# A planner's DMA rate, a tie between weight loads, and the order of three engines

## The chip, the cores and the metric

The kernel runs on one core of a Trainium2 chip. The metric is the device time of the whole launch in microseconds, lower is better. The kernel was timed three times; the profile is of one more execution, taken by the hardware profiler. Engines are called by the profile's names: PE (TensorE), DVE (VectorE), ACT (ScalarE), POOL (GpSimd) and SP (SyncE, which issues nearly all DMA transfers).

## The reference

A causal attention with a cumulative bias feeds a first MLP (softplus) and that feeds a second one (a rational function of its hidden values):

```
scores = q @ k.T / sqrt(64)                     # 4 batches x 8 heads, 576 x 576
bias   = -(cum[:, None] - cum[None, :])         # cum = cumsum(max(s, 0))
attn   = softmax(causal(scores + min(bias, 0)))
x      = (attn @ v) as [2304, 512]
h = x @ w_in;  g = softplus(h);  x = g @ w_out              # MLP 1, d_ff 2048
h = x @ w_in2; g = P(h) / (Q(h) + 1e-6); y = g @ w_out2     # MLP 2, P cubic, Q in |h| and h^2
```

The result must hold fp32 accuracy, so every large product is three matmuls on values that are split into a high and a low fp32r part (high by high, high by low, low by high).

## The kernel before, in words

**Tiling.** MLP 1 goes over six tiles of tokens (256, 256, then four of 448), and each tile over 16 blocks of 128 hidden values. One such block of one tile is a unit: `stage_a` makes `h` in a PSUM bank by 12 matmuls (L1093, L1094, L1095), `stage1` turns it into softplus (Exp at L1191 and Ln at L1192 on ACT, the last step `e <- e, h` at L1194 on DVE), `stage3` splits the result into `gh` (L1395) and `gl` (L1397), and `stage_b` multiplies these by the output weights three units later (L1129 to L1131). There are **two banks for `h`** (`N_H = 2`), so the matmuls of a unit wait for the L1194 of the unit two before it. That wait is where the first engine of this kernel, PE, meets DVE.

**Weights.** They come in as 64-bit words. `load_w` (L895) brings half a block, 512 KB, into a buffer `raw64` (two of them) or into one half of `raw64x`; `conv_t` turns it into fp32 (DVE L908, ACT L909, DVE L910, output `tc`), and `conv_hl` splits it (ACT L914, POOL L915). The low halves of MLP 1's input weights don't fit and are kept in DRAM: `stream_l` (L934) loads one of them, `w1l`, 256 KB, for each half unit. While the last tile of MLP 1 runs (about 470 to 640 us) the weights of MLP 2 are loaded and converted, and parts of them are stored to DRAM again (`store_a`, L1014, 256 KB each, and L993, 512 KB each). The first tile of MLP 2 needs MLP 1's output back from DRAM as `yt` (`load_y`, L1072; first ACT step on it L1061).

**The start.** The attention's q and k come by L509 into tiles `raw2` of 64 partitions (256 KB each), v by L520, and two rows of the cumulative sum, `cumc`, are added to a q/k tile by L513; the first matmuls on them are L619.

**The order.** A planner, `class Planner`, walks over all instructions with a model of each engine and lists them engine by engine in the order in which they would start. `plan` repeats that a few times with ranks from the last pass and keeps the best, and at the end of the kernel each instruction up to a planned time of 936 us is tied behind its predecessor on its engine. So the order of PE, DVE, ACT, POOL and of SP's DMA issues is the planner's, and it is fixed: an engine that comes to an instruction whose input is late waits, with all that stands behind it.

The planner's model of a transfer is one server for all queues: it takes the bytes by `DMA_RATE`, adds a latency of 1.9 us, and lets no more than 8 transfers be open at once:

```
if s.dma:
    dma = max(dma, clock[s.engine]) + s.dma / DMA_RATE
    self.after[k] = dma + DMA_LATENCY - self.end[k]
    landed.append(dma + DMA_LATENCY)
```

`queue_behind(last, k0)` ties the instructions that were issued since `k0` behind the ones in `last`, each on its own engine, whatever the planner would like.

Of the kernel before, what the change touches and what calls it, by code (L numbers as in the profile page):

```python
# [67 lines left out]
          ("wide", "two"): 0.2, ("wide", "one"): 0.05, ("thin", "two"): 0.6, ("thin", "one"): 0.3}  # L68
HOLD, ROUNDS = 0.0, 6
UNTIL = 936.0  # L70
DMA_RATE, DMA_LATENCY, LANES = 320e3, 1.9, 8


class Access:
# [34 lines left out]
class Step:  # L109


    def __init__(self, i, tied):
        self.i, self.tied = i, tied
        self.engine = str(i.engine).split(".")[-1]
        acc = [[Access(x) for x in xs if getattr(getattr(x, "bass_ap", None), "tensor", None) is not None]
               for xs in (i.outs, i.ins)]
        self.outs, self.ins = acc
        self.dma, self.port = 0, None
        n = self.outs[0].elements if self.outs else 1
        psum = any(x.psum for x in self.outs + self.ins)  # L120
        wide = len(self.ins) > 1 and self.ins[1].dims[1][1] > 1
        if "DMA" in i.opcode:
            self.dma = 4 * n * self.outs[0].dims[0][1]
            self.busy = self.done = ISSUE.get(self.engine, 0.5)
        elif self.engine == "PE":
            turn = self.ins[0].tile.startswith("ident")
            full = not turn and "32r" not in str(i.ins[0].bass_ap.dtype)
            self.busy = 0.00085 * n if turn else 0.024 + 0.00162 * n if full else 0.012 + 0.000428 * n
            self.done = self.busy + 0.165
        elif self.engine == "Activation":  # L130
            more = max(0, len(self.outs) + len(self.ins) - 2)
            near = any(x.psum for x in self.ins)
            self.busy = (0.12 + 0.00079 * n + 0.07 * more) if near else (0.165 + 0.0008 * n + 0.095 * more)
            self.done = self.busy + 0.08
        elif self.engine == "DVE" and n == 1:
            self.busy, self.done = 0.115, 0.155
        elif self.engine == "DVE":
            one = len(self.ins) < 2 and not psum and i.opcode != "TensorCopy"
            self.busy = 0.06 + 0.00064 * n if one else 0.107 + 0.00105 * n
            self.done = self.busy + 0.06  # L140
            self.port = None if psum else "one" if one else "two"
        elif self.engine == "Pool":
            self.busy = 0.22 + 0.00205 * n if wide else 0.28 + 0.0007 * n
            self.done = self.busy + 0.03
            self.port = "wide" if wide else "thin"
        else:
            self.busy = self.done = 0.1
# [39 lines left out]
class Planner:  # L187
# [27 lines left out]
    def forward(self, rank):  # L215
        steps, tiles, pool, queue = self.steps, self.tiles, self.pool, self.queue
        n = len(steps)
        open_ = [len(p) for p in self.preds]
        left = {t: len(u) for t, u in self.users.items()}
        slots = {tag: [(0.0, None)] * bufs for tag, bufs in pool.values()}  # L220
        head = {tag: 0 for tag in slots}
        last = {tag: 0.0 for tag in slots}
        held, freed = set(), {}
        ready = [0.0] * n
        self.start, self.end, self.after = [0.0] * n, [0.0] * n, [0.0] * n
        self.slot_of = {}
        clock = {e: 0.0 for e in self.engines}
        port = {e: None for e in self.engines}
        wait = {e: [k for k, s in enumerate(steps) if s.engine == e and not open_[k]] for e in self.engines}
        self.lines = {e: [] for e in self.engines}  # L230
        dma, landed = 0.0, []

        def earliest(k):
            t, need = ready[k], {}
            if steps[k].dma and len(landed) >= LANES:
                t = max(t, landed[-LANES])
            for x in tiles[k]:
                if x not in held:
                    tag = pool[x][0]
                    need[tag] = need.get(tag, 0) + 1  # L240
                    ahead = queue[tag][head[tag]:head[tag] + need[tag]]
                    if any(y not in held and y not in tiles[k] for y in ahead):
                        return None
                    free = sorted(slots[tag], key=lambda q: q[0])
                    if len(free) < need[tag]:
                        return None
                    t = max(t, free[need[tag] - 1][0], last[tag])
            return t

        for _ in range(n):  # L250
            best = None
            for e in self.engines:
                can = [(max(t, clock[e]), rank[k], k) for k in wait[e] for t in (earliest(k),) if t is not None]
                if can:
                    t0 = min(can)[0]
                    pick = min((c for c in can if c[0] <= t0 + HOLD), key=lambda c: (c[1], c[0], c[2]))
                    if best is None or pick[0] < best[0]:
                        best = pick
            t, _, k = best
            s = steps[k]  # L260
            wait[s.engine].remove(k)
            for x in tiles[k]:
                if x not in held:
                    tag = pool[x][0]
                    slots[tag].sort(key=lambda q: q[0])
                    self.slot_of[x] = slots[tag].pop(0)[1]
                    held.add(x)
                    last[tag] = max(last[tag], t)
                    while head[tag] < len(queue[tag]) and queue[tag][head[tag]] in held:
                        head[tag] += 1  # L270
            busy, done = s.busy, s.done
            if s.port:
                other = "Pool" if s.engine == "DVE" else "DVE"
                slow = SHARED.get((s.port, port[other]), 0.0) * max(0.0, min(clock[other] - t, busy))
                busy, done = busy + slow, done + slow
            port[s.engine] = s.port
            self.start[k], clock[s.engine] = t, t + busy
            self.end[k] = t + busy
            if s.dma:
                dma = max(dma, clock[s.engine]) + s.dma / DMA_RATE  # L280
                self.after[k] = dma + DMA_LATENCY - self.end[k]
                landed.append(dma + DMA_LATENCY)
            else:
                self.after[k] = done - busy
            done = self.end[k] + self.after[k]
            self.lines[s.engine].append(k)
            for j, result in self.succ[k]:
                at = self.end[k] + self.lag(k, j) if result else t
                ready[j] = max(ready[j], at)
                open_[j] -= 1  # L290
                if not open_[j]:
                    wait[steps[j].engine].append(j)
            for x in tiles[k]:
                left[x] -= 1
                freed[x] = max(freed.get(x, 0.0), done)
                if not left[x]:
                    slots[pool[x][0]].append((freed[x] + 0.04, x))
        return max(self.end)
# [41 lines left out]
def moe_chain_kernel(ctx, tc, qk0, v0, qk, vv, s0, s, w1, w2, ab, out):  # L340
    nc = tc.nc
# [103 lines left out]
    def queue_behind(last, k0):  # L445
        for i in traced(k0):
            if i.engine in last:
                after(i, last[i.engine])
# [385 lines left out]
    n = 0  # L834
# [47 lines left out]
    xs_t = {}  # L882
    h_t, g_t, acc_t = {}, {}, {}
    raw64 = {}

    def load_w(m, ff, half, al=None):
        n = c2.index((ff, half)) if m else 0
        if n % 2:
            if "x" not in raw64:
                raw64["x"] = t_x("raw64x", [128, 2, 512, 2], I32)  # L890
            r = raw64["x"][:, n // 2 % 2]
        else:
            r = (al or t_r)("raw64", [128, 512, 2], I32)
        src = (w1, w2)[m][ff, :, half * 512:(half + 1) * 512].bitcast(I32)
        nc.sync.dma_start(out=r.rearrange("p a b -> p (a b)"), in_=src)  # L895
        raw64[m, ff, half] = r

    def conv(m, ff, half, hi, lo):
# [502 lines left out]
    if True:  # L1401
# [54 lines left out]
        for n in range(n_st):  # L1456
            if n == 1:
                last = {i.engine: i for i in traced()}
                k0 = len(nc.cur_bb.bb.instructions)
# [60 lines left out]
        for i in range(NU):  # L1520
# [41 lines left out]
            if u is not None:  # L1562
# [7 lines left out]
                if t4 >= 34 and t4 % 2 == 0 and FS + (t4 - 34) // 2 < NF:  # L1570
                    reload2(FS + (t4 - 34) // 2)
                if ph == 0 and T == 3 and ff == 8:
                    nc.sync.dma_start(out=abt, in_=ab)
                    nc.vector.memset(qc, QC)
                    nc.vector.tensor_scalar(nega, abt[:, 0:4], -1.0, None, op0=ALU.mult)
                    nc.scalar.activation(babs, abt[:, 4:6], AF.Abs)
                if ph == 0 and T == 5 and ff == 8:
                    load_y(0)
                if ph == 1:
# [102 lines left out]
```

## Time and profile before

| | |
|---|---|
| Three timed runs, median (lowest, highest) | 1022.59 us (1021.87, 1023.67) |
| The profiled execution's own time | 1024.62 us |
| Its span, first to last instruction | 1022.7 us |
| Mean granted clock of TensorE | 1.000 of full speed |
| PE busy | 998.6 us, 98% of the span |
| DVE, ACT, POOL busy | 789.9 us, 763.7 us, 469.1 us |
| Bytes moved by DMA | 201.62 MB, a mean of 197 GB/s |

PE is the engine to look at. Its busy time leaves 24.1 us of the span, and the other engines and the DMA queue matter where they make PE wait. The profiled execution is 2.0 us above the median of the three timed runs; the span is within 0.1 us of it.

### The profile page before, as it was taken

The numbers are of one execution on the slowest core, as the hardware profiler recorded it, in microseconds if no ns is written. First come the engines' busy times: TensorE is split into PE (matmuls) and PEld (weight loads), VectorE is DVE, ScalarE is ACT, GpSimd is POOL, SyncE is SP. The second block draws the span as 40 slices with busy tenths as digits, with TensorE's granted clock in tenths as the row PEclk, the third lists the DMA queues.
The fourth block names the chain that finished last, engine by engine and source line by source line (L and its number), as shares of the span: only waits on it lengthen the run. The fifth ranks groups of instructions, "written<-read, shape, count | busy, mean of one in ns | idle before, by whom it ended". The sixth has DMA issues, their size and how long they took to land.

```text
span 1022.7 us, 18157 instructions
## 1 busy us (share of the span) xinstructions
PE 998.6 (98%) x5924; PEld 904.1 (88%) x5924; DVE 789.9 (77%) x1783; ACT 763.7 (75%) x1556; POOL 469.1 (46%) x464
## 2 busy tenths in 40 slices
PE   6989999999999999999999999999999999999998
PEld 5789999988999888899999999888888898889897
DVE  5799887877886887887677658887788778777765
ACT  5998777776885776776566667788779878788775
POOL 2776664411221112221446665676466457555542
PEclk9999999999999999999999999999999999999999
DMA  9778565474554654335999998628456656655300
GB/s 254 294 235 289 188 207 182 157 225 150 166 173 149 198 161 125 116 108 175 357 350 328 303 334 295 207 83 285 158 165 196 213 168 195 209 161 168 124 1 31
DMA packets 101069, 201.62 MB, mean 197 GB/s; under 512 B 11248, under 2 KB 30512, under 8 KB 100976
## 3 DMA queue, kind: packets, MB, share of 16 engines
q1 hardware_dynamic: 98432, 196.31, 58.6%
q10 hardware_dynamic: 2544, 4.16, 1.6%
q8 instruction: 47, 0.77, 0.3%
q14 instruction: 46, 0.38, 0.1%
HBM read 161.16 MB, written 35.19 MB: 192 GB/s over the span
## 4 chain that ended last, share of the span: by engine, by line
PE 87%; DVE 4%; DMA 3%; ACT 2%; POOL 2%; issue 1%; SPq 0%; POOLq 0%; DVEq 0%; ACTq 0%
PE h L1094 6%; PE at L1340 6%; PE h L1093 6%; PE h L1095 6%; PE at L763 5%; PE acc L1131 5%; PE acc L1130 5%; PE acc L1129 5%; PE h L1340 5%; PE acc L1270 4%; PE acc L1269 4%; PE acc L1271 4%; PE at L622 2%; PE at L623 2%; PE acc L1136 2%; PE acc L1137 2%
## 5 line engine op out<-in xcount | busy, mean ns | idle before, releaser
L615 POOL TENSOR_SCALAR PA<-PA,stat 128x384 f32<-128x384 f32 (+3 forms) x112 | 69.9, 629 | 179.7 <-DVE stat L614 113.4
L1093 PE MATMUL h<-xs,w1h 128*128 128x448 f32 (+1 forms) x360 | 122.9, 342 | 0.8 <-DVE stat L613 0.7
L1095 PE MATMUL h<-xs,w1l 128*128 128x448 f32 (+1 forms) x360 | 122.6, 342 | 0.9 <-DMA w1l<-l_d 0.8
L1094 PE MATMUL h<-xs,w1h 128*128 128x448 f32 (+1 forms) x360 | 122.6, 341 | 0.0
L1130 PE MATMUL acc<-gl,w1h 128*128 128x448 f32 (+1 forms) x352 | 119.3, 340 | 0.8 <-POOL gl L1397 0.8
L1131 PE MATMUL acc<-gh,w1l 128*128 128x448 f32 (+1 forms) x352 | 118.3, 339 | 0.3 <-POOL w1l L915 0.2
L1129 PE MATMUL acc<-gh,w1h 128*128 128x448 f32 (+1 forms) x352 | 118.4, 338 | 0.0
L1255 POOL TENSOR_TENSOR gl<-PA,gh 128x512 fp32r<-128x512 f32 x48 | 63.2, 1319 | 68.0 <-issue 51.7
L612 ACT ACTIVATE PA<-PA,stat 128x384 f32<-128x384 f32 (+3 forms) x112 | 63.9, 572 | 21.6 <-DVE stat L595 20.4
L1269 PE MATMUL acc<-w2b,gh 128*128 128x512 f32 x192 | 76.0, 396 | 0.0
L1270 PE MATMUL acc<-w2b,gh 128*128 128x512 f32 x192 | 75.8, 395 | 0.0
L1271 PE MATMUL acc<-w2b,gl 128*128 128x512 f32 x192 | 73.5, 394 | 0.0
L1093 PEld LDWEIGHTS h<-xs,w1h 128*128 128x128 f32 x360 | 68.0, 189 | 4.6 <-ACT pt L673 0.9
L1095 PEld LDWEIGHTS h<-xs,w1l 128*128 128x128 f32 x360 | 67.7, 188 | 4.8 <-DMA w1l<-l_d 1.0
L1094 PEld LDWEIGHTS h<-xs,w1h 128*128 128x128 f32 x360 | 67.9, 188 | 3.3
L1191 ACT ACTIVATE e<-h 128x448 f32<-128x448 f32 (+1 forms) x90 | 43.5, 483 | 36.2 <-PE h L1095 34.4
L1130 PEld LDWEIGHTS acc<-gl,w1h 128*128 128x128 f32 x352 | 66.2, 188 | 4.2 <-POOL gl L1397 1.0
L1131 PEld LDWEIGHTS acc<-gh,w1l 128*128 128x128 f32 x352 | 66.1, 188 | 3.6 <-POOL w1l L915 0.4
L1129 PEld LDWEIGHTS acc<-gh,w1h 128*128 128x128 f32 x352 | 66.2, 189 | 3.2
L1397 POOL TENSOR_TENSOR gl<-e,gh 128x256 fp32r<-128x256 f32 (+1 forms) x48 | 48.0, 1002 | 29.9 <-ACT gh L1395 21.0
L595 DVE CUSTOM_DVE_ANT_0 PA<-at,mask 128x384 f32<-128x384 f32 (+3 forms) x100 | 50.2, 519 | 7.4 <-PE at L623 5.0
L622 PE MATMUL at<-ht 128*128 128x512 f32 (+3 forms) x156 | 53.3, 347 | 0.1
(352 smaller groups left out, 3141.9 us busy)
## 6 DMA issues: line engine op xcount, KB each, us to landing
wa<-wa_d SPq DMA_DIRECT2D x100, 512.0 KB
w1l<-l_d SPq DMA_DIRECT2D x138, 256.0 KB
raw<-in_w_dram SPq DMA_DIRECT2D x48, 512.0 KB
raw<-in_qk_dram SPq DMA_DIRECT2D x24, 384.0 KB
l_d<-w1l SPq DMA_DIRECT2D x32, 256.0 KB
raw64x<-in_w_dram SPq DMA_DIRECT2D x16, 512.0 KB
wa_d<-pt SPq DMA_DIRECT2D x16, 512.0 KB
raw<-in_qk_dram SPq DMA_DIRECT2D x8, 576.0 KB
```

Source lines behind the costliest of these rows:

```text
L615: nc.gpsimd.tensor_scalar(pt[:, 0:n], pt[:, 0:n], stat[:, i, 2:3], 1.0, op0=ALU.mult, op1=ALU.mult)
L622: nc.tensor.matmul(o, hq, p.ht[:, 1, k0:k0 + n], start=True, stop=False)
L1093: nc.tensor.matmul(h, wh[:, cs], xh, start=(k == 0), stop=False)
L1094: nc.tensor.matmul(h, wh[:, cs], xl, start=False, stop=False)
L1095: nc.tensor.matmul(h, wl[:, cs], xh, start=False, stop=(k == KD - 1))
L1129: nc.tensor.matmul(o, wh[:, cs], gh, start=first and not both, stop=False)
L1130: nc.tensor.matmul(o, wh[:, cs], gl, start=False, stop=False)
L1131: nc.tensor.matmul(o, wl[:, cs], gh, start=False, stop=last and (not both or m % 2 == 1))
L1269: nc.tensor.matmul(acc[m], gh[:, cs], wh, start=first, stop=False)
L1270: nc.tensor.matmul(acc[m], gh[:, cs], wl, start=False, stop=False)
L1271: nc.tensor.matmul(acc[m], gl[:, cs], wh, start=False, stop=last)
L1340: nc.tensor.matmul(o[:, p * 256:p * 256 + 256], x, z[:, k], start=first and p == k == n == 0, stop=(k, n) == (1, 2), skip_group_check=True)
```

## The change

The planner's model of a transfer is changed in three ways: the rate goes from 320e3 to 400e3 bytes per us; a transfer whose tile in SBUF spans at most 64 partitions counts its bytes double; and a transfer that ACT issues (only the stores of `ht`) no longer queues behind SP's, but takes its own doubled bytes and the latency. Two ties are added: every `load_w` stands behind the `load_w` before it in program order (in both MLPs, since both call it), and the load of MLP 2's parameters `ab` with the three small instructions that follow it stands behind what was issued ahead of it.

```diff
-DMA_RATE, DMA_LATENCY, LANES = 320e3, 1.9, 8
+DMA_RATE, DMA_LATENCY, LANES = 400e3, 1.9, 8
...
         if "DMA" in i.opcode:
-            self.dma = 4 * n * self.outs[0].dims[0][1]
+            near = [x for x in self.outs + self.ins if x.pool]
+            rows = near[0].box[1] - near[0].box[0] if near else 128
+            self.dma = 4 * n * self.outs[0].dims[0][1] * (1 if rows > 64 else 2)
...
-            if s.dma:
+            if s.dma and s.engine != "SP":
+                self.after[k] = 2 * s.dma / DMA_RATE + DMA_LATENCY
+                dma += s.dma / DMA_RATE
+            elif s.dma:
                 dma = max(dma, clock[s.engine]) + s.dma / DMA_RATE
...
         src = (w1, w2)[m][ff, :, half * 512:(half + 1) * 512].bitcast(I32)
+        k0 = len(nc.cur_bb.bb.instructions)
         nc.sync.dma_start(out=r.rearrange("p a b -> p (a b)"), in_=src)
+        queue_behind(w_last, k0)
+        w_last.update({i.engine: i for i in traced(k0)})
...
                 if ph == 0 and T == 3 and ff == 8:
+                    last = {i.engine: i for i in traced()}
+                    k0 = len(nc.cur_bb.bb.instructions)
                     nc.sync.dma_start(out=abt, in_=ab)
                     nc.vector.memset(qc, QC)
                     nc.vector.tensor_scalar(nega, abt[:, 0:4], -1.0, None, op0=ALU.mult)
                     nc.scalar.activation(babs, abt[:, 4:6], AF.Abs)
+                    queue_behind(last, k0)
```

No instruction is added or taken away on any engine; what changes is the order. It changes in two stretches of the program, the first 300 us and about 450 to 660 us, and a little on PE between 700 and 740 us. Line numbers move too: of the lines named here L513 becomes L518, L895 becomes L902, L908 and L910 become L917 and L919, L934 becomes L943, L1014 becomes L1023, L1061 becomes L1070, L1072 becomes L1081, L1191 becomes L1200 and L1194 becomes L1203.

**First place, SP at the start.** The queue of transfers of before, from the seventh on (`v2` is the first batch's v, `raw64` is weight words, `prm` the parameters `ab`, `raw2` q and k, `cumc` the cumulative sums):

```order
L520 DMA v2_137<-in_v0_dram 128x1536
L895 DMA raw64_1799<-in_w1_dram 128x1024
L895 DMA raw64_1937<-in_w1_dram 128x1024
L1573 DMA prm_123<-in_ab_dram 128x6
L513 DMA raw2_131<-cumc_147 2x1024
L513 DMA raw2_133<-cumc_147 2x1024
L513 DMA raw2_135<-cumc_147 2x1024
```

The same place of the change:

```order
L525 DMA v2_137<-in_v0_dram 128x1536
L518 DMA raw2_131<-cumc_147 2x1024
L518 DMA raw2_133<-cumc_147 2x1024
L518 DMA raw2_135<-cumc_147 2x1024
L514 DMA raw2_321<-in_qk0_dram 64x1024
L518 DMA raw2_321<-cumc_147 2x1024
L902 DMA raw64_163<-in_w1_dram 128x1024
```

Two weight loads of 512 KB, which belong to the 23rd and 24th half blocks, and the parameters no longer stand ahead of the `cumc` rows; the two loads now stand at the 85th and 86th place of the queue.

**Second place, SP and ACT around 550 us.** SP's queue of before from the load of `w1l_7231` on (`raw64x` and `raw64` are weight words of MLP 2, `wa_d` the DRAM copy of its converted weights, `yt` MLP 1's output read back in two pieces, `y_d0` and `y_d256`):

```order
L934 DMA w1l_7231<-l_d4_0_72 128x512
L934 DMA w1l_7233<-l_d0_1_65 128x512
L895 DMA raw64x_6483<-in_w2_dram 128x1024
L934 DMA w1l_7293<-l_d5_0_74 128x512
L1072 DMA yt_7602<-y_d0_112 128x4x256
L934 DMA w1l_7295<-l_d1_1_67 128x512
L895 DMA raw64_7240<-in_w2_dram 128x1024
```

The same loads in the change:

```order
L943 DMA w1l_7231<-l_d4_0_72 128x512
L902 DMA raw64x_6483<-in_w2_dram 128x1024
L1023 DMA wa_d2_0_104<-w2a_7095 128x2x256
L943 DMA w1l_7233<-l_d0_1_65 128x512
L1023 DMA wa_d2_1_105<-w2a_7154 128x2x256
L1081 DMA yt_7602<-y_d256_113 128x4x128
L943 DMA w1l_7293<-l_d5_0_74 128x512
L1023 DMA wa_d2_0_104<-w2a_7095 128x2x256
L943 DMA w1l_7295<-l_d1_1_67 128x512
L902 DMA raw64_7240<-in_w2_dram 128x1024
L1023 DMA wa_d2_1_105<-w2a_7154 128x2x256
```

Four stores of `w2a`, 256 KB each, have come in between the loads here, from 60 to 70 places further back; the second piece of `yt` stands ahead of `w1l_7293`, where it stood 13 places behind it. ACT's order of before in the same stretch (`e` and `h` belong to the units of MLP 1's last tile):

```order
L914 ACTIVATE PA_7209<-tc_7181 128x512
L909 ACTIVATE raw64x_6483<-raw64x_6483 128x512
L1191 ACTIVATE e_7255<-h_7242 128x448
L1192 ACTIVATE e_7255<-e_7255 128x448
L914 ACTIVATE PA_7259<-tc_7235 128x512
```

And of the change:

```order
L1404 ACTIVATE gh_7269<-e_7199 128x448
L1070 ACTIVATE yt_7602<-yt_7602 128x384
L1070 ACTIVATE xs_7809<-yt_7602 128x384
L918 ACTIVATE raw64x_6483<-raw64x_6483 128x512
L1200 ACTIVATE e_7255<-h_7242 128x448
L1201 ACTIVATE e_7255<-e_7255 128x448
```

Two steps that read `yt`, and so wait for both of its pieces, stand ahead of the Exp of unit `h_7242`; before they stood three units later, on either side of the Exp of `h_7414`.

**Third place, DVE around 580 us.** DVE's order of before, from unit `h_7466` on (`tc` is the output of the conversion of MLP 2's weights):

```order
L1194 SCALAR_TENSOR_TENSOR e_7479<-e_7479,h_7466 128x448
L1167 COPY yb_7289<-acc_6515 128x448
L908 TENSOR_SCALAR tc_7409<-raw64_7240 128x512
L910 SCALAR_TENSOR_TENSOR tc_7409<-raw64_7240,tc_7409 128x512
L1194 SCALAR_TENSOR_TENSOR e_7524<-e_7524,h_7511 128x448
L908 TENSOR_SCALAR tc_7460<-raw64x_6483 128x512
L910 SCALAR_TENSOR_TENSOR tc_7460<-raw64x_6483,tc_7460 128x512
L1194 SCALAR_TENSOR_TENSOR e_7570<-e_7570,h_7557 128x448
L908 TENSOR_SCALAR tc_7506<-raw64_7360 128x512
L1194 SCALAR_TENSOR_TENSOR e_7618<-e_7618,h_7605 128x448
```

The same instructions in the change:

```order
L917 TENSOR_SCALAR tc_7409<-raw64_7240 128x512
L919 SCALAR_TENSOR_TENSOR tc_7409<-raw64_7240,tc_7409 128x512
L917 TENSOR_SCALAR tc_7460<-raw64x_6483 128x512
L919 SCALAR_TENSOR_TENSOR tc_7460<-raw64x_6483,tc_7460 128x512
L917 TENSOR_SCALAR tc_7506<-raw64_7360 128x512
L1203 SCALAR_TENSOR_TENSOR e_7479<-e_7479,h_7466 128x448
L919 SCALAR_TENSOR_TENSOR tc_7506<-raw64_7360,tc_7506 128x512
L917 TENSOR_SCALAR tc_7551<-raw64x_6483 128x512
L919 SCALAR_TENSOR_TENSOR tc_7551<-raw64x_6483,tc_7551 128x512
L917 TENSOR_SCALAR tc_7597<-raw64_7464 128x512
L1203 SCALAR_TENSOR_TENSOR e_7524<-e_7524,h_7511 128x448
```

The first step of the conversion of `raw64_7360` stood behind the last step of unit `h_7557` and now stands ahead of that of unit `h_7466`, three units earlier; the conversions behind it have moved by three units or more.

## Rows read from the trace of the kernel before

**Rows 1.** The page, part 1: busy time and share of the span of each engine.

```profile
PE 998.6 (98%) x5924; PEld 904.1 (88%) x5924; DVE 789.9 (77%) x1783; ACT 763.7 (75%) x1556; POOL 469.1 (46%) x464
```

**Rows 2.** The core by stretches: us, busy time of each engine, clock, DMA share, GB/s.

```profile
0.00:200.00 200.00, 183.56 (x1309) 170.53 (x1309) 160.32 (x493) 153.17 (x374) 115.70 (x139) 1.00 0.68 224
450.00:700.00 250.00, 250.00 (x1292) 229.30 (x1291) 182.12 (x303) 173.28 (x334) 136.20 (x113) 1.00 0.78 261
700.00:800.00 100.00, 97.93 (x611) 86.83 (x610) 81.45 (x119) 80.83 (x136) 57.09 (x44) 1.00 0.63 209
1000.00:1022.70 22.70, 18.86 (x89) 15.70 (x87) 13.04 (x24) 12.60 (x24) 6.83 (x7) 1.00 0.10 35
```

**Rows 3.** What PE waited for, 0 to 16 us: us in all, times, longest.

```profile
PE acc L619 <- DMA raw<-in_qk_dram: 4.9, 1, 4.9
...
PE at L619 <- DMA raw<-cumc: 1.1, 1, 1.1
```

**Rows 4.** The chain that ended last, at the start: start us, us, what.

```profile
7.74 5.88 DMA raw<-cumc
```

**Rows 5.** SP's issues at the start: start us, us, engine, line, transfer.

```profile
4.21 0.58 SPq L520 DMA_DIRECT2D v<-in_v_dram  x1
4.84 0.91 SPq L895 DMA_DIRECT2D raw<-in_w_dram  x2
5.79 0.43 SPq L1573 DMA_DIRECT2D prm<-in_ab_dram  x1
7.74 1.96 SPq L513 DMA_DIRECT2D raw<-cumc  x3
```

**Rows 6.** The core by stretches, as in rows 2, by what the DMA engines moved.

```profile
40.00:45.00 5.00, 4.94 (x36) 4.44 (x35) 3.71 (x20) 4.55 (x16) 2.46 (x5) 1.00 1.03 411
...
460.00:480.00 20.00, 20.00 (x117) 18.14 (x117) 13.48 (x35) 13.01 (x29) 2.35 (x4) 1.00 0.45 151
480.00:500.00 20.00, 20.00 (x99) 18.39 (x98) 15.08 (x25) 12.60 (x24) 7.86 (x6) 1.00 0.98 326
500.00:520.00 20.00, 20.00 (x99) 18.38 (x99) 12.63 (x19) 12.05 (x23) 9.27 (x7) 1.00 1.02 371
520.00:540.00 20.00, 20.00 (x100) 18.38 (x99) 16.08 (x28) 13.57 (x26) 9.27 (x7) 1.00 0.97 337
540.00:560.00 20.00, 20.00 (x100) 18.38 (x99) 16.42 (x21) 12.00 (x22) 12.17 (x10) 1.00 0.97 324
560.00:580.00 20.00, 20.00 (x100) 18.43 (x99) 11.50 (x18) 12.58 (x25) 12.67 (x11) 1.00 0.93 299
580.00:600.00 20.00, 20.00 (x100) 18.43 (x99) 11.79 (x15) 13.10 (x24) 12.21 (x10) 1.00 0.98 331
```

**Rows 7.** SP: the first and the last of nine stores that the change brings forward.

```profile
565.60 0.43 SPq L1014 DMA_DIRECT2D wa_d<-w2a  x1
...
633.08 0.99 SPq L1014 DMA_DIRECT2D wa_d<-w2a  x1
```

**Rows 8.** PE at the first matmul of a unit, around 559 us.

```profile
558.90 0.36 PE L1093 MATMUL h<-xs,w1h 128*128 128x448 f32 x1
```

**Rows 9.** ACT around 553 us.

```profile
552.04 0.67 ACT L909 ACTIVATE raw64x<-raw64x 128x512 f32<-128x512 f32 x1
553.03 0.55 ACT L1191 ACTIVATE e<-h 128x448 f32<-128x448 f32 x1 [0.31 <-PE h L1095]
553.61 0.58 ACT L1192 ACTIVATE e<-e 128x448 f32<-128x448 f32 x1
```

**Rows 10.** SP's issues from 543 us.

```profile
543.56 0.45 SPq L895 DMA_DIRECT2D raw64x<-in_w_dram  x1
545.60 0.32 SPq L934 DMA_DIRECT2D w1l<-l_d  x1
...
558.72 0.56 SPq L1072 DMA_DIRECT2D yt<-y_d  x1
```

**Rows 11.** DVE from 574 to 589 us, with the idle time ahead and its releaser.

```profile
574.13 0.62 DVE L1194 SCALAR_TENSOR_TENSOR e<-e,h 128x448 f32<-128x448 f32 x1
...
576.43 1.36 DVE L908 TENSOR_SCALAR tc<-raw 128x512 int32<-128x512 int32 x1 [1.15 <-POOL pt L991]
577.90 0.69 DVE L910 SCALAR_TENSOR_TENSOR tc<-raw,tc 128x512 int32<-128x512 int32 x1
...
584.57 1.14 DVE L908 TENSOR_SCALAR tc<-raw 128x512 int32<-128x512 int32 x1 [0.37 <-DMA raw<-in_w_dram]
588.52 0.62 DVE L1194 SCALAR_TENSOR_TENSOR e<-e,h 128x448 f32<-128x448 f32 x1 [2.81 <-ACT e L1192]
```

**Rows 12.** SP's issue of the load that DVE waits for at 584.57.

```profile
578.62 0.33 SPq L895 DMA_DIRECT2D raw<-in_w_dram  x1
```

**Rows 13.** PE at the first matmul of two units, around 580 and 589 us.

```profile
579.69 0.37 PE L1093 MATMUL h<-xs,w1h 128*128 128x448 f32 x1
...
588.64 0.37 PE L1093 MATMUL h<-xs,w1h 128*128 128x448 f32 x1
```

More of the change, by code (lines that the diff above doesn't have):

```diff
@@ L884, in moe_chain_kernel @@
     raw64 = {}
+    w_last = {}
     def load_w(m, ff, half, al=None):
```

## The prediction, made before the changed kernel ran

> **What bounds the kernel now.** I read the page's busy times first: PE works 998.6 of 1022.7 us, and no other engine is above 77% [rows 1]. So the time is PE's work plus its idle time, 24.1 us, and since the change adds and removes no instruction, only idle time can move. The second view is the core by stretches: PE is idle for 16.4 us in the first 200 us, for nothing at all between 450 and 700 us, for 2.1 us between 700 and 800, and for 3.8 us at the very end [rows 2]. That frames what the change can do. In its first stretch there is idle time to win. In its second, 450 to 660 us, there is none: whatever is late there comes on top, and behind it PE is so full that little is won back.
>
> The third view is the engines' timelines at the places where the order moves: which instruction an engine comes to, and what that instruction waits for. The granted clock is full in all stretches, so no term hangs on it.
>
> **The start.** PE's first matmuls wait 4.9 us for q and k, which the change leaves alone, and then 1.1 us for the `cumc` rows [rows 3]. In the chain that ended last these rows take 5.88 us from their issue at 7.74 to landing at 13.62 [rows 4]. They are tiny; the time is that of what was issued shortly ahead of them: v, two weight loads of 512 KB and the parameters [rows 5]. The change takes the two weight loads and the parameters from ahead of them, 1.05 MB. The best rate that the queue shows is 411 GB/s [rows 6], by which that is 2.6 us. The gain is at least 1.1 us, the wait that a transfer ends, if something else is late next (the next matmuls need the following q/k tile, which also comes earlier), and at most about 2.6 us. I take 2. The tie of the parameter load and its three instructions costs nothing by itself: they are needed by MLP 2 only and move to near 400 us, and their load is 3 KB. The two weight loads are the 23rd and 24th half blocks; at their new place, the 85th and 86th of the queue, they still come in the order of their use.
>
> **The second stretch, DMA.** The planner books every transfer here at 400 instead of 320 GB/s, since weight words, `w1l` and the stores all span 128 partitions. The trace says what the queue gives when it is full: shares of 0.93 to 1.02, and 299 to 371 GB/s from 480 to 600 us, about 330 on average [rows 6]. So 320 was close, and 400 is a fifth too fast, in the one stretch where the queue is full for over 100 us. The planner thinks it has room and fills it: nine 256 KB stores of `w2a` come forward from between 565.6 and 633 us [rows 7] into the queue of about 520 to 565 us, and the second weight load of some pairs from later or idler places. Counted in SP's order from the first load of MLP 2's weights to the load of `raw64_7360`, 107 transfers of 37.55 MB now stand where 99 of 35.19 MB stood. The 2.36 MB more are 7.3 us at the 324 GB/s of 540 to 560 us. As there was no gap in the queue, up to 7.3 us is how much later this load lands.
>
> The Trainium skill speaks against my reading here: its HBM Reference, section Specifications, gives about 425 GB/s for a core that streams alone, and a share of about 358 when two do. By 425 the planner's 400 would be right and the extra bytes would take 5.6 us, booked in full by the plan. The trace reaches 411 for 5 us, but no 20 us of this stretch gets above 371, so I keep the rows; what the page's figure would make of the kernel is the first rival.
>
> **The second stretch, DVE.** This is the term that decides. A unit's matmuls reuse the PSUM bank of the unit two before, so `h_7557` waits for L1194 of `h_7466`. Before, that step ran at 574.13, 5.6 us ahead of PE's need at 579.69 [rows 11, 13], and the conversion of `raw64_7360` came only after three more units, at 584.57, where DVE already waited 0.37 us for the load [rows 11]. In the change that conversion stands directly ahead of L1194 of `h_7466`. If the load lands just when it did, DVE takes it at 584.57, needs 1.14 us, then 0.62 us for the unit's step [rows 11], done at 586.3: `h_7557` starts 6.6 us late. If the load is also 7.3 us later by the extra bytes, 13.9 us late.
>
> Can it land earlier? It was issued at 578.62 [rows 12], as soon as L910 at 577.90 (0.69 us) had read the buffer that it goes into [rows 11]. That L910 and its L908 may now run up to some 3.5 us earlier, since they stand ahead of `h_7466`'s step and need not wait 1.15 us for POOL if its order helps. Issued at 575 and with the same 5.95 us to landing, it gives 581.0 + 1.8 = 582.8, 3 us late; only with a transfer at the booked rate (1.3 us plus the model's 1.9 us) is it 578.2 + 1.8, 0.3 us late, practically on time. So this term lies between 0 and 13.9. I take 12: the queue is full, so the extra bytes count for most of their 7.3 us, and the next units, up to `h_7651` (588.64 before [rows 13]), each have a further load's conversion ahead of their bank's step, so a late queue hits them too.
>
> **The second stretch, ACT.** Two steps on `yt` now stand ahead of `h_7242`'s Exp, which ran at 553.03 [rows 9]. They need the second piece of `yt`, issued at 558.72 before; now it stands ahead of the `w1l` load of 545.60 [rows 10] but behind the extra stores. Issued between 545.6 and 553 (the queue's delay), and with about 6 us to landing as for `raw64_7360`, it lands at 551.6 to 559. Then the two steps (0.55 each, taken as the Exp's), L909 (0.67), Exp (0.55), Ln (0.58) [rows 9] and DVE's 0.62 are 3.5 us, so the bank of `h_7362`, wanted at 558.90 [rows 8], is free at 555.1 to 562.5: 0 to 3.6 us late. This is no second sum: while PE stands, the queue goes on, and the DVE stall shrinks by as much. It counts in full only if SP is held up too; I put it at 0, and its 3.6 us into the top of the range.
>
> **The sum.** −2 at the start, +12 in the second stretch; PE is 100% busy behind it until 700, and can win back at most its 2.1 us of 700 to 800 [rows 2], which I leave out. Against the profiled execution (span 1022.7, own time 1024.62) that is +10. The median of the timed runs, 1022.59, is 2.0 us under that execution's own time; on it the same +10 is **1032.6 us**. Its own bounds: −2.6 + 6.6 − 2.1 gives 1024.5, and −1.1 + 13.9 + 3.6 gives 1039.0; with some room for what stands behind the late loads, 1025 to 1041.
>
> **Rivals.**
>
> *The loads land as planned.* If the queue gives 400 GB/s once the plan asks for it, conversions are on time, nothing is late at 580, and the start's 1.1 to 2.6 us stay: 1020 to 1021.5; with a little more of the 16.4 us of idle time of the first 200 us, 1018. For it: 411 in one window, and that the move relieves the end of the stretch. It decides if `raw64_7360` lands before 577.9, that is 1.14 and 0.62 us ahead of 579.69. Against it: the queue was already full, with eight transfers open, and gave 330.
>
> *A small stall.* The chain of issues and frees moves forward with the order, the load lands 3 us earlier, and the stall of 0 to 4 us cancels the gain: 1020.5 to 1024.6. It needs SP, DVE and POOL to be early together.
>
> *SP is held up as well.* SP issues in order. A `w1l` load waits for a buffer that PE frees, a weight load for one that DVE frees; if PE stands for DVE, these issues stand too, and the next weight loads behind them come late again. A second delay of the size of the first makes +22 − 2: 1042 or more.
>
> *The model is better, and the first 300 us gain more.* Transfers of 64 partitions are now priced apart; if PE's 16.4 us there shrink by 6, the sum is +6, still slower: inside the range.
>
> **Chances.** Forecast with its own range, 0.66; loads as planned, 0.17; small stall, 0.07; SP held up, 0.10. Changes below 0.2%, 2 us, are about what can't be told from none here (the three runs span 1.8 us). Faster: the first rival and a sliver of the second, 0.18; same, the second's rest, 0.05; slower, 0.77. The range leaves out the last rival's 0.10 and the lower part of the first: **1019 to 1041**.
>
> **What would show it.** The start: PE's wait for `cumc` gone, first L619 matmul of the chain about 2 us earlier. DMA: still 300 to 370 GB/s and a share near 1 from 480 to 600. DVE: L917 on `raw64` waits for DMA several us around 580 to 600, and PE, which was never idle there, waits for DVE's L1203 or for `w1l`, some 12 us in all. It is wrong if PE stays full from 450 to 700, or if its idle time there is far beyond 14 us; the DMA rate in that stretch tells which step failed.

## The result, and the profile after

The changed kernel takes **1036.88 us** (median of 4 runs, 1036.45 to 1038.1) against 1022.57 us of before: **+14.3 us, a ratio of 1.0143** (95% interval 1.0128 to 1.0158). It is slower, as forecast, and by more than the +10 of the sum, inside its range. The two parts of that sum came out quite differently from what the text above says, and that is what the rest is about.

The profiled execution took 1036.47 us, with a span of 1034.7; the first line of the page's part 1:

```profile
PE 1000.0 (97%) x5924; PEld 902.2 (87%) x5924; DVE 793.8 (77%) x1783; ACT 765.6 (74%) x1556; POOL 472.6 (46%) x464
```

PE's idle time is 34.7 us now, 10.6 more than in [rows 1]; the busy time is 1.4 us longer, and together that is the 12.0 us by which the two spans differ. The medians differ by more, 14.3 us, since the profiled execution of before was 2.0 us above its median and that of the change 0.4 us below. The stretches of PE, in the columns of [rows 2] and [rows 6]:

```profile
0.00:200.00 200.00, 177.96 (x1282) 164.64 (x1283) 162.03 (x484) 151.06 (x368) 115.09 (x136) 1.00 0.68 220
...
540.00:560.00 20.00, 18.93 (x89) 16.28 (x89) 12.28 (x20) 11.46 (x22) 11.79 (x9) 1.00 1.04 372
560.00:580.00 20.00, 15.43 (x69) 13.78 (x69) 12.57 (x19) 11.73 (x23) 10.42 (x9) 0.91 0.97 347
580.00:600.00 20.00, 20.00 (x100) 18.48 (x99) 12.72 (x17) 13.38 (x25) 12.74 (x11) 1.00 1.00 372
700.00:800.00 100.00, 98.18 (x615) 87.71 (x615) 80.95 (x118) 80.65 (x137) 63.40 (x48) 1.00 0.60 192
```

Three things are to be read here against [rows 2]. The first 200 us hold 22.0 us of PE idle time where 16.4 were: the stretch that was to win 2 us loses 5.6, of which 1.1 come back by 300 us. From 540 to 580 PE stands 5.6 us, where it never stood before. And the clock of 560 to 580 is 0.91. The DMA queue moves 372, 347 and 372 GB/s where [rows 6] have 324, 299 and 331.

Of these 5.6 us, 1.1 are three short waits between 544 and 551; the rest is one wait, at 565.3 to 569.9. PE's timeline there, with the idle time ahead of an instruction and what ended it (the chain is then followed back, engine by engine):

```profile
569.87 0.74 PE L1138 MATMUL acc<-gh,w1h 128*128 128x448 f32 x1 [4.57 <-ACT yb L1174]
570.41 0.57 PE L1139 MATMUL acc<-gl,w1h 128*128 128x448 f32 x1
570.78 0.57 PE L1140 MATMUL acc<-gh,w1l 128*128 128x448 f32 x1
...
573.00 0.37 PE L1102 MATMUL h<-xs,w1h 128*128 128x448 f32 x1
573.21 0.36 PE L1103 MATMUL h<-xs,w1h 128*128 128x448 f32 x1
```

PE waits 4.57 us for a PSUM bank that ACT's copy `yb` empties. ACT's timeline there:

```profile
560.36 0.53 ACT L1070 ACTIVATE yt<-yt 128x384 fp32r<-128x384 f32 x1 [3.69 <-DMA yt<-y_d]
...
569.27 0.54 ACT L1174 ACTIVATE yb<-acc 128x448 f32<-128x448 f32 x1 [3.46 <-DVE tc L919]
```

That copy waits 3.46 us for a DVE conversion, since `yb` goes into the buffer of the weight words that it reads. DVE:

```profile
566.97 1.34 DVE L917 TENSOR_SCALAR tc<-raw 128x512 int32<-128x512 int32 x1 [2.29 <-POOL PA L924]
...
568.56 0.68 DVE L919 SCALAR_TENSOR_TENSOR tc<-raw,tc 128x512 int32<-128x512 int32 x1
...
593.12 1.30 DVE L917 TENSOR_SCALAR tc<-raw 128x512 int32<-128x512 int32 x1 [0.47 <-DMA raw<-in_w_dram]
...
596.88 0.43 DVE L917 TENSOR_SCALAR tc<-raw64x 128x512 int32<-128x512 int32 x1 [1.33 <-DMA raw64x<-in_w_dram]
```

The conversion waits for POOL, 2.29 us, to free a `tc`. POOL:

```profile
565.67 1.26 POOL L924 TENSOR_TENSOR PA<-tc,PA 128x512 fp32r<-128x512 f32 x1 [5.35 <-DMA wa_d<-PA]
```

POOL waits 5.35 us for a **store**, that of `PA`, to leave its buffer. In before POOL's waits for such a store, 540 to 600 us, were (us in all, times, longest):

```profile
POOL PA L915 <- DMA wa_d<-PA: 0.6, 1, 0.6
```

SP's issues in the change ahead of that store, the row at 559.60:

```profile
552.00 0.37 SPq L1023 DMA_DIRECT2D wa_d<-w2a  x1
...
554.99 0.37 SPq L1023 DMA_DIRECT2D wa_d<-w2a  x1
...
558.23 0.37 SPq L1023 DMA_DIRECT2D wa_d<-w2a  x1
...
559.60 0.37 SPq L1023 DMA_DIRECT2D wa_d<-PA  x1
```

Three stores of `w2a` that stood far behind in before are now issued ahead of it (552.00, 554.99 and 558.23), at a DMA share of 1.04. So the chain is store of `PA`, POOL, DVE, ACT, PE. The waits of DVE for the loads of `raw64`, which were to decide, are also there, 0.47 and 1.33 us at 593.12 and 596.88, but PE doesn't stand for them: it runs some 10 us later by then.

### The profile page after: what moved, and what is told of

Its sections match the earlier page's. It is cut to its first block, busy times and chain, and to the rows that moved or that the text cites. A ratio compares the mean times of both kernels' runs of the same rounds, so it can differ in the third digit from the quotient of the medians.

```text
span 1034.7 us, 18179 instructions
## 1 busy us (share of the span) xinstructions
PE 1000.0 (97%) x5924; PEld 902.2 (87%) x5924; DVE 793.8 (77%) x1783; ACT 765.6 (74%) x1556; POOL 472.6 (46%) x464
## 5 line engine op out<-in xcount | busy, mean ns | idle before, releaser
L1200 ACT ACTIVATE e<-h 128x448 f32<-128x448 f32 (+1 forms) x90 | 43.3, 481 | 31.0 <-PE h L1104 26.8
L924 POOL TENSOR_TENSOR w1l<-tc,w1h 128x512 fp32r<-128x512 f32 x32 | 45.3, 1422 | 27.0 <-PE acc L1140 13.5
```

## Experiments

Each ratio is to runs of the kernel before on the same chip, with its 95% interval; the microseconds behind it are the ratio times 1022.57 us. Since the planner orders everything at once, a change of one number moves both stretches. So several of the kernels make the plan twice, by the old and by the new model, and join the two: the cut is where the same instructions lie ahead in both, near a planned 440 us on each engine.

```diff
+    made = {m: best_lines(instructions, both if m == "after" else tied, m) for m in {EARLY, LATE}}
...
+        p = min(cuts[e], key=lambda c: abs(c[1] - CUT[2]))[0]
+        out.append([i for i, t in a[:p]] + [i for i, t in b[p:] if t < until])
```

**1. The two stretches apart.** `EARLY, LATE = "after", "before"` is early_only, the other way round late_only.

> Every engine's order is the change's up to a planned 440 us and that of before behind it; the sets of instructions on either side are the same in both. Theory (the two stretches add up): the 4.5 us of PE idle time that the trace of the change shows more in the first 300 us are all there, 1027 us, and nothing in the stretch from 540 us. Rival (as predicted for the start): the cumc rows come earlier and 2 us are won, 1020.6. Second rival: what is lost early is won back later, 1022 to 1023.

Measured: 1.0046 (1.0032 to 1.0060), +4.7 us. The early theory holds, and the rival, my own term for the start, falls. PE's first 200 us hold 23.1 us of idle time where [rows 2] have 16.4. The largest part of the difference lies between 120 and 160 us, 4.1 us where before has 0.9 (early_only, then before):

```profile
120.00:160.00 40.00, 35.88 (x276) 34.44 (x276) 31.09 (x82) 27.64 (x63) 22.48 (x23) 1.00 0.62 196
120.00:160.00 40.00, 39.06 (x305) 38.08 (x306) 31.53 (x90) 30.10 (x69) 22.75 (x25) 1.00 0.62 202
```

> The other half: the order of before up to 440 us, the change's behind it. Theory: PE stands 5.6 us at 540 to 580, 0.8 us at 640 to 700, and its clock falls behind the stall (1.4 us): +7.8, 1030.4. Rival (as predicted): the stall is 12 us, 1034.6. The two halves together should give the change's +14.3.

Measured: 1.0078 (1.0049 to 1.0107), +8.0 us, as the first theory has it; the 12 of my sum lie outside the interval (5.0 to 10.9). The halves give 12.7, the change 14.3, within their intervals. The stall is the same one, 4.2 us for the `yb` copy, and the stretches by windows show the DMA share near 1 and the clock again:

```profile
PE acc L1166 <- ACT yb L1202: 4.2, 1, 4.2
...
540.00:560.00 20.00, 18.16 (x88) 16.07 (x86) 12.28 (x21) 12.20 (x24) 11.39 (x9) 1.00 1.05 385
560.00:580.00 20.00, 17.68 (x76) 16.18 (x77) 13.95 (x19) 11.88 (x23) 14.19 (x11) 0.83 0.94 325
580.00:600.00 20.00, 20.00 (x101) 18.46 (x100) 13.95 (x17) 13.06 (x25) 12.41 (x10) 1.00 1.03 397
```

**2. Which part of the change.** Edits: the rate put back in the change; the rate alone in before; the two ties alone; the double count and ACT's transfers alone.

```diff
-DMA_RATE, DMA_LATENCY, LANES = 400e3, 1.9, 8
+DMA_RATE, DMA_LATENCY, LANES = 320e3, 1.9, 8
```

> The change with the planner's rate put back to 320e3; both ties, the double count and ACT's own transfers stay. Theory (the rate overbooks the queue from 480 us on): no stall at 540 to 580, and 1022 to 1028 depending on the early order. Rival (the tie between the weight loads of the second MLP forces the loads and stores): the stall stays, 1030 or more.

Measured: 0.9974 (0.9962 to 0.9987), 2.7 us **faster** than before. No stall: PE is busy throughout from 540 to 600 us, and the queue is back at 309 to 319 GB/s.

```profile
540.00:560.00 20.00, 20.00 (x100) 18.38 (x99) 12.74 (x17) 11.38 (x21) 10.48 (x8) 1.00 0.90 309
560.00:580.00 20.00, 20.00 (x100) 18.44 (x99) 11.68 (x17) 12.39 (x25) 13.46 (x12) 1.00 0.94 319
```

> The kernel before with the rate alone at 400e3. Theory: the stall at 540 to 580 is there as in the change, 6 to 8 us, 1029 to 1032 with an early order of its own. Rival (the ties make the stall): 1022 to 1024.

Measured: 1.0148 (1.0124 to 1.0172), +15.1 us: as slow as the whole change, slower than I expected. PE waits 5.6 us for the `yb` copy again, and at the start 6.6 us for `cumc`: the rate alone leaves the two weight loads at the queue's head, while it puts PE's matmul on `cumc` ahead of the transposes that PE could do first.

```profile
PE acc L1129 <- ACT yb L1165: 5.6, 1, 5.6
...
PE at L619 <- DMA raw<-cumc: 6.6, 1, 6.6
```

> The kernel before with the two ties alone: rate 320e3, no double count, ACT's transfers as before. rate_undone was 0.26% faster than before. Theory (the tie that keeps weight loads in order gives that, by the start): 1020 to 1021. Rival (the double count gives it, the tie nothing): 1022 to 1025.

Measured: 1.0005 (0.9996 to 1.0014), no change; the theory falls. The ties do take the two weight loads out of the head of the queue, but PE's order has the matmul on `cumc` ahead of the transposes here, as in the change, and PE waits for it longer than the 1.1 us of [rows 3]:

```profile
PE at L621 <- DMA raw<-cumc: 3.2, 1, 3.2
```

> The kernel before with the double count for 64 partitions and ACT's own transfers alone: rate 320e3, no ties. From 440 us on the order is that of before. ties_alone changed nothing and rate_undone, with both, gained 0.26%. Theory (the double count gives the gain, by the order of the first 300 us): 1020 to 1021. Rival (only both together give it, since the ties take the two weight loads out of the head of the queue): 1022 to 1025.

Measured: 1.0010 (1.0000 to 1.0020), no gain. In its profile the clock fell to 0.92 from 20 to 40 us, which costs 1.6 us; but PE's idle time up to 300 us isn't lower than in before either, 19.1 against 17.9 us. So the rate alone makes the loss, and neither of the other parts alone makes the gain of rate_undone; only together do they. In rate_undone the loads are gone from the head of the queue, PE has the transposes first, and it doesn't wait for `cumc`.

The Trainium skill, on its page SBUF — State Buffer, section Door 1: The DMA port swizzle, lets 64 partitions reach half the ports of 128 and so half the bandwidth, as the new model has it. The trace of before agrees. These are its GB/s from 5 to 30 us, in slices of 0.625 us; by SP's order (q and k are issued ahead of v, the weight loads behind it [rows 5]) the second to fourth slice, 197 to 203 GB/s, are q and k with 64 partitions, and the eighth to twelfth, 393 to 413, mainly the weight loads with 128:

```profile
GB/s 223 197 203 203 246 236 423 393 413 406 406 393 339 223 229 328 400 360 354 220 188 198 251 265 397 429 334 190 180 204 216 200 229 285 363 391 419 420 413 400
```

True as it is, the double count won nothing alone.

**3. What stalls at 565.** Both kernels are late_only with one thing put back to its place in before, in the final lists of the planner.

```diff
+    slots_as("before", "SP", lambda t: t and "w2a" in t[-1])
```

> As late_only, but the 16 stores of w2a stand at the places of SP's queue that they have in before; all else of the change's order from 440 us on stays. Theory (the stores brought forward delay what stands behind them in the queue: the second piece of yt, and the store of PA that POOL waits 4.95 us for): most of the 8 us go, 1023 to 1025.5. Rival (the new order of DVE, ACT and POOL waits by itself): the stall stays, 1029 or more.

Measured: 1.0025 (1.0013 to 1.0038), +2.6 us instead of 8.0. The stores are two thirds of it; POOL doesn't wait for a store any more, ACT not for `yt`, and PE's longest wait for the `yb` copy is 1.4 us. What causes the last 2.6 us was not taken apart; by stretches PE is idle for 1.4, 0.4 and 0.6 us at 540 to 580, 580 to 640 and 640 to 700, where before has no idle time. PE's longest wait, 540 to 600 us (us in all, times, longest):

```profile
PE acc L1188 <- ACT yb L1224: 1.4, 1, 1.4
```

```diff
+    for e in ("Activation", "DVE"):
+        place_as("before", e, lambda t: len(t) > 1 and "yt_7602" in t[1:] and t[0] in ("yt_7602", "xs_7809"))
```

> As late_only, but ACT's two first steps on yt (and the one on DVE) stand where before has them, ahead of and behind the Exp of h_7414. Theory (the chain to PE's 4.2 us wait runs from the store of PA over POOL, DVE and ACT's yb copy, and ACT's 3.25 us wait for yt only lies beside it): the stall stays nearly whole, 1029 to 1031. Rival (ACT's wait for yt starts the lateness): 1023 to 1026.

Measured: 1.0089 (1.0074 to 1.0104), +9.1 us: nothing won. ACT's wait for `yt` was 3.69 us long in the change, the longest of ACT's in this stretch, and cost nothing. With it gone, POOL still waits for the store of `PA`, and PE for `yb`:

```profile
559.78 1.26 POOL L975 TENSOR_TENSOR PA<-tc,PA 128x512 fp32r<-128x512 f32 x1 [4.95 <-DMA wa_d<-PA]
```

```profile
PE acc L1189 <- ACT yb L1225: 4.7, 1, 4.7
```

**4. The start.** In the kernel before, only the two weight loads are moved, to the 88th and 89th place of the queue.

```diff
+    place_as("after", "SP", lambda t: t and t[0] in ("raw64_1799", "raw64_1937"))
```

> The kernel before in its own order, but for the two weight loads at the 8th and 9th place of SP's queue, which go to the 88th and 89th, in the order of the loads. Theory (as predicted for the start): cumc lands up to 2.6 us sooner, 1.1 to 2.6 us are won, 1020.0 to 1021.5. Rival (PE's next wait takes its place, as in the change, whose idle time up to 20 us is not lower): 1022.6, no change.

Measured: 0.9979 (0.9970 to 0.9987), −2.1 us. The term of the prediction is right by itself; PE's wait for `cumc` of [rows 3] is gone. So what happened to it in the change? PE's head there:

```profile
11.18 0.77 PE L624 MATMUL at<-raw 66*128 66x128 f32 x2 [3.49 <-DMA raw<-cumc]
11.73 0.85 PE L699 MATMUL acc<-ident,gh 128*128 128x128 f32 x3
```

And in before:

```profile
9.87 0.90 PE L694 MATMUL acc<-ident,gh 128*128 128x128 f32 x3 [2.04 <-POOL gh L615]
...
13.66 1.65 PE L619 MATMUL at<-raw 66*128 66x128 f32 x4 [1.09 <-DMA raw<-cumc]
```

The matmul on `cumc` starts 2.5 us sooner, at 11.18 instead of 13.66, but the plan has put it ahead of the transposes (L699, before L694), so these now wait too; PE waits 3.49 us in one piece, where it waited 2.0 and 1.1 us.

> As early_only, but on PE the first two matmuls on the tile that cumc completes stand behind the six transposes again, as in before. In early_only PE waits 3.28 us for cumc with the transposes behind it, which were ready 1.3 us sooner. Theory (the head of PE's queue eats the earlier landing): idle time up to 20 us falls from 8.7 to about 7, and 1 to 1.5 us are won against early_only, 1026 to 1027. Rival (it only moves the wait): idle time up to 20 us stays at 8.5 or more.

Measured: 1.0053 (1.0035 to 1.0071) against early_only's 1.0046: PE's idle time up to 20 us falls from 8.7 to 6.9, as the theory says, but no gain was measured. The intervals, +3.6 to +7.2 us against +3.2 to +6.0, leave room for the theory's 1 to 1.5 us. In the profiles PE's idle time falls by 3.7 us in all (29.8 to 26.1), while its busy time grows by 3.0 us (996.7 to 999.7); why it grows is not shown.

```profile
0.00:20.00 20.00, 11.31 (x46) 9.21 (x47) 11.40 (x55) 9.70 (x29) 6.75 (x21) 1.00 0.77 222
0.00:20.00 20.00, 13.08 (x42) 10.69 (x43) 10.89 (x50) 10.00 (x28) 7.13 (x21) 1.00 0.79 224
```

The edit of the next one takes three splits of weights (POOL) from ahead of softmax scalings:

```diff
+    for x, y in [("w1l_2107", "P4_1457"), ("w1l_1308", "PA_1094"), ("w1l_2403", "P4_1770")]:
+        line["Pool"].remove(at[x])
+        line["Pool"].insert(line["Pool"].index(at[y]) + 1, at[x])
```

> As early_only, but on POOL three splits of w1l (of w1l_1308, w1l_2107 and w1l_2403) stand behind the softmax scalings that they stand ahead of in the change. In early_only POOL waits 2.95 us at one of them for a buffer that PE frees, and PE then waits 1.2 us for the scaling behind it. Theory: PE's waits for POOL's scalings at 120 to 150 us go, idle time at 120 to 160 falls from 4.1 to about 2, and the kernel gains 1 to 2 us on early_only, 1025.5 to 1027. Rival (the waits come from DVE and ACT ahead of POOL): idle time there stays at 3.5 or more.

Measured: 1.0085 (1.0064 to 1.0107), slower than early_only. PE's wait for the scaling at 130 us goes, but a longer one stands in its place, for DVE, and idle time of 120 to 160 us goes from 4.1 to 5.6, as the rival has it; behind that wait the clock falls too, to 0.96 over the stretch, which costs about 1.6 us more:

```profile
133.11 0.44 PE L680 MATMUL at<-ht 128*128 128x384 f32 x1 [2.72 <-DVE pt L733]
```

Neither of my two readings of what makes the 4.7 us of the first 300 us is thus shown as a cause: the move on POOL made it worse, and of the move on PE no gain was measured. It stays open which of the moves makes them.

**5. A better version.** The order of rate_undone early, that of before late.

```diff
+MODELS = {"before": (320e3, 1, False), "mid": (320e3, 2, True)}
+EARLY, LATE, CUT = "mid", "before", (420, 460, 440)
```

> The order of rate_undone up to a planned 440 us and that of before behind it. rate_undone has 2 us less idle time than before up to 450 us and 2 us more from 640 to 800. Theory (the two add up): 1018 to 1020, faster than both. Rival: what is saved early is not kept, 1020.5 to 1022.

Measured: **0.9955** (0.9939 to 0.9971), median 1019.87 us, 4.6 us faster than before. On that chip before took 1023.70 us. The ratio is below those of rate_undone (0.9974) and start_loads (0.9979), but its interval overlaps the first and touches the second, so that it is faster than both is not shown beyond the noise. Idle time moved as the theory has it, 16.5 us up to 450 and 2.1 from 640 to 800, where before has 18.2 and 2.1 and rate_undone 16.1 and 4.0. But that is 1.6 us: the other 3.2 of the 4.8 us between the profiled spans are busy time (995.4 against 998.6), which the theory doesn't explain.

## Why the prediction was right, and where not

**The bound.** Right for the change: of the 12.0 us between the spans 10.6 are idle time, and what came on top from 450 to 700 was not won back. That "only idle time can move" is too strong, though. The same 5924 matmuls are busy for 995.4 us (best_mix) to 1001.0 us (late_yt_back) in the profiles here, in part by the clock.

**The start, −2.** The price of the move is right (start_loads, −2.1). As a term of the sum it failed: early_only is +4.7. The step at fault: I priced one row of SP's queue and took the rest of the first 300 us for unchanged, though the order of PE and POOL there had moved as well; the prediction named only a rival by which these moves would *gain*. It is the largest error, 6.7 us. Of what the prediction said would show it, the first matmul on `cumc` did come about 2 us earlier, but PE's wait for `cumc` was not gone; it was 3.49 us.

**The queue.** The direction is right, and the rate is the cause of both losses: PE's idle time is 16.0 us up to 300 us and none at 540 to 580 in rate_undone, 25.8 and 5.6 in rate_alone, 17.9 and none in before. The number is not: "as there was no gap in the queue" it was to give the 324 GB/s of [rows 6], but it gave 372 and 347, and up to 397 in late_only. So at a share of 0.93 to 0.98 there was room: from 540 to 560 the GB/s of before dip to 160 in slices of 0.5 us, those of the change to no less than 277. Nor did it reach the booked 400 where the stall arose, and PE stood: the first rival, loads landing as planned, falls too. The 425 GB/s that the Trainium skill (HBM Reference, Specifications) gives for a core that streams alone were not reached in any 20 us here; 399 are the most (late_yt_back, 580 to 600).

**The stall, +12 at `h_7557` by DVE.** This step failed in place and mechanism, and its size was half too large: late_only is +8.0. PE waited neither for DVE's L1203 nor for `w1l`, as forecast, but 4.57 us for ACT's `yb` copy. The late transfer that counted was not a load in front of DVE but a store: POOL could not reuse `PA`'s buffer, and the lateness went over POOL, DVE and ACT to a bank that `stage_b` needs, 14 us ahead of where I looked. The stores of `w2a`, which I counted only as bytes ahead of a load, are two thirds of it (late_stores_back puts all 16 back).

**ACT's wait for `yt`.** The second piece was predicted to land at 551.6 to 559; ACT waited for it and started at 560.36. Putting it at 0 in the sum was right (late_yt_back), though for another reason than that DVE's stall would cover it.

**What the sum left out: the clock.** The prediction read a full clock in before and hung no term on it. Behind the 4.57 us wait the granted clock falls to half; by the stretches below that costs 1.5 us.

So direction and range were right, but the total came near by luck: two errors of opposite sign, +6.7 us at the start and −4.0 in the second stretch, cancel in part. The rest of the 14.3, 1.6 us, is within the intervals of the two halves.

## What to carry to other kernels

A rate in a planner is a promise to every engine. Where transfers come later than booked, an engine can stand for a store's buffer as well as for a load's data; here it was the store. So follow the buffers that stores free too, not only the data that are loaded. And if a number sets the order of a whole program, price the order of every stretch that moves, or measure the stretches apart, before adding up single rows; a wait that a row shows may vanish and the time not move (late_yt_back).

## What the runs showed of the hardware

In the change TensorE's granted clock fell behind the wait of 4.57 us. In the 14 us before that wait PE had not stood at all, and from 540 to 551 for 1.1 us in three short waits. The stretches behind it (the clock stands ahead of the DMA share and the GB/s):

```profile
570.00:572.00 2.00, 2.00 (x6) 1.78 (x7) 0.77 (x2) 1.49 (x3) 1.59 (x2) 0.50 0.98 376
572.00:574.00 2.00, 2.00 (x9) 1.81 (x8) 1.51 (x2) 1.15 (x2) 1.76 (x2) 0.76 0.52 172
574.00:576.00 2.00, 2.00 (x11) 1.85 (x11) 1.44 (x3) 1.44 (x3) 2.00 (x2) 1.00 0.97 353
```

From 570 to 572 it is 0.50, the lower of the two levels (1.2 of 2.4 GHz), and two matmuls start 0.37 us apart (570.41, 570.78) where it is 0.21 at full clock (573.00, 573.21). From 574 on it is 1.00 again. Against full clock the two stretches lose 1.0 and 0.5 us. In late_only, behind a wait of 4.2 us, the clock of 560 to 580 is 0.83. In the change's first 200 us, where the waits behind PE's first matmul are 3.49 us and less, it stays at 1.00; in early_pool_back, with a wait of 2.72 us at 133, it is 0.96 from 120 to 160; and in double_alone it is 0.50 from 20 to 22 us and 0.68 from 22 to 24, behind waits of 1.63 and 0.68 us between 15.9 and 19.4. So the length of the longest wait alone does not settle whether it falls.

The DMA queue, with a share of 0.94 to 1.05, moves between 325 and 397 GB/s in stretches of 20 us (late_only), and at the same share of 0.97 it moves 324 GB/s in before (540 to 560) and 347 in the change (560 to 580). So a share near 1 doesn't tell how much more it can take. The mix differs: the 20 us of late_only with 397 GB/s issue loads alone, those with 325 issue 10 loads and 11 stores. How much of the difference is the mix was not taken apart.
